# Last layer B of a four-layer kernel: the row gather moved into layer A's inverse, and the last results returned block by block

## The chip, the cores and the metric

The kernel runs on one core of a Trainium2 chip. The metric is the device time of one execution in microseconds (us). Five engines are named as in the profile: PE (TensorE, the matrix engine; PEld is its loading of weights), DVE (VectorE), ACT (ScalarE), POOL (GpSimd) and SP (SyncE). SP does no arithmetic and issues most of the DMA transfers; ACT issues some. Each engine runs its own list of instructions in order, and so does a queue of transfers: an issue that has to wait holds back whatever stands behind it on the same engine.

## What is computed

Four layers run one after the other on x, with 2048 rows of 512 channels: A, B, A, B, each on a layer norm of x and added to it.

```python
x = x + _A_ref(_layernorm(x), A_w_r, A_w_i)      # irfft2(rfft2(x) * W)
x = x + _B_ref(_layernorm(x), ...)               # long convolution of each channel
x = x + _A_ref(_layernorm(x), A_w_r, A_w_i)
x = x + _B_ref(_layernorm(x), ...)

# _B_ref, for each channel d of 512, L = 2048:
K = einsum("dn,dnl,dn->dl", Cc, exp(dt * A * l), dt * Bc).real
y = irfft(rfft(pad(u, 2 * L)) * rfft(pad(K, 2 * L)))[:L] + u * Dskip
```

The kernel does the transforms as matrix products in two steps, because 2048 is split into 128 x 16. The first index is called s1 and lies on the 128 partitions; the second, s2, counts 16 places.

## The kernel before

Layer B of pass r (r = 0 the first layer B, r = 1 the last one) works on two halves e of the channels, 256 each. It has three steps, and between them the data pass through HBM, since each step wants another index on the partitions.

1. `forward_b(r, b, e)`, eight blocks b of two s2 values each: normalise (DVE, L505), transform along s1 (PE, L761), copy from PSUM (ACT, L779) into a buffer of the ring `iy`, and write the rows to the HBM tensor `yd[r][e]` (L782, on SP or ACT).
2. `group_b(r, q, e)`, eight groups q: load the kernel's spectrum `khat` (L865), load the group's rows from `yd` into a buffer of the ring `yi` (L868), transform along s2 (`spectrum`, PE, L803), multiply by the spectrum (DVE, L880, four products), add (POOL, L886, two sums), transform back along s2 (PE, L895), copy (ACT, L904, four copies), and write to the HBM tensor `vd[r][e]` (L905, on ACT).
3. `inv_b(r, b, e)`, eight blocks b: load from `vd` into a buffer of the ring `iy` (L914, on SP), transform back along s1 (PE, L920), add to x (DVE, L926), and in the last layer store the result (L944, one half on SP and one on ACT).

`yd` and `vd` have 8 x 4 x 2 x 2 x 16 x 2 x 256 places, called q, i, a, c, s, w, d. The four indices q, i, a, c together are the partition (128) of steps 1 and 3; a, c, s, w together are that of step 2. So step 1 and step 3 see `pieces`, all partitions and a few s, and step 2 sees `block`, one q:

```python
def pieces(t, b):
    return t.rearrange("q i a c s w d -> (q i a c) s w d")[:, 2 * b:2 * b + 2]
def block(t, q):
    return t[q].rearrange("i a c s w d -> (a c s w) i d")
```

A group therefore needs the rows of all eight blocks of its half, and an inverse block needs all eight groups.

Layer A's second pass ends with sixteen pieces `inv_a(1, s2)` (PE, L730 and L738), with which the sixteen `forward_b(1, b, e)` are interleaved.

The order of all instructions is set by a planner, `Clock.run`: every piece of work is a generator with a rank; at each `yield` it names the engine and the buffers that it needs next, and the events it waits for (`after` an event's planned time, or once it is `emitted`); the planner takes the ready piece of the lowest rank by its own planned times. Buffers are slices of big SBUF tensors: `Ya` (8192 floats in each partition), `Y` (16384), `wk`, `apart`. In pass 1 of layer B, `Ya` holds the rings `yi` and `vo` (four buffers of 1024 floats each), and the second half of `Y` is free by then.

## Time and profile before

| | |
|---|---|
| time, median of 3 runs | 831.39 us (831.05 to 833.83) |
| profiled execution, its own time | 832.5 us |
| its span | 830.7 us |
| mean granted clock of PE | 0.871 |
| PE, DVE, ACT, POOL busy | 625.7, 509.0, 419.8, 279.2 us |
| HBM read, written | 103.47 MB, 60.69 MB |
| transfers Ya<-yd (step 2's loads, both layers B) | 32 of 512 KB, median 10.9 us from issue to landing |
| transfers vd<-Ya | 32 of 512 KB, 6.8 us |
| transfers wk<-vd | 32 of 512 KB, 4.8 us |

Times in the profile count from the span's start. In a row of instructions, `Ya<-yd` reads: written to Ya, read from yd; "x8" is a count. Matrix products in 32-bit floats appear twice in the profile's counts, so that an inverse block's four products are eight records. "To landing" is the time from a transfer's issue to its completion. A wait "A <- B" is idle time of engine and line A, ended by B; "issue" stands where the profile shows nothing that was waited for.

### The profile page before, as it was taken

Reading aid. Unit: us, or ns where it says so; the run is one execution under the profiler, and the core shown is the slowest. Engines: PE = TensorE matmul, PEld = TensorE weight load, DVE = VectorE, ACT = ScalarE, POOL = GpSimd, SP = SyncE. Lnnn points to the kernel's source line nnn. Section 1 sums busy time; section 2 is a strip of 40 time slices with the busy share of each in tenths; the row PEclk is TensorE's granted clock in tenths of the full one; section 3 lists DMA queues with packets and bytes.
Section 4 is the critical chain, followed back from the end, with each engine's and each line's share of the span. In section 5 each row is a group of like instructions: output and inputs, shape, how many; then the busy total and the mean of one; then the engine's idle time right before and its main releaser. Section 6 shows DMA issues by size and latency. Waiting matters only on the chain. (4 is left out here: it accounts for less than half of the span.)

```text
span 830.7 us, 19222 instructions
## 1 busy us (share of the span) xinstructions
PE 625.7 (75%) x7716; PEld 365.4 (44%) x7716; DVE 509.0 (61%) x1019; ACT 419.8 (51%) x755; POOL 279.2 (34%) x275
## 2 busy tenths in 40 slices
PE   4388888678699888885866765699877999577755
PEld 3277555345465333431322322377766534143322
DVE  5966577847757766871432724785877587474533
ACT  5676898888788676752233122085542244332110
POOL 4381345524634411400332404084533000083420
PEclk9699899989899899996686869789997999896776
DMA  9324213623525845399899996600656233799997
GB/s 324 115 86 137 98 44 87 187 84 83 165 68 159 258 148 162 112 347 347 255 332 287 391 386 228 244 0 14 230 203 212 91 124 128 259 323 378 334 309 224
DMA packets 127256, 165.40 MB, mean 199 GB/s; under 512 B 7260, under 2 KB 102240, under 8 KB 127040
## 3 DMA queue, kind: packets, MB, share of 16 engines
q1 hardware_dynamic: 80768, 122.23, 44.4%
q10 hardware_dynamic: 46400, 41.95, 14.8%
q8 instruction: 61, 1.00, 0.5%
q14 instruction: 27, 0.22, 0.1%
HBM read 103.47 MB, written 60.69 MB: 198 GB/s over the span
## 5 line engine op out<-in xcount | busy, mean ns | idle before, releaser
L1131 POOL TENSOR_TENSOR Y<-wk,Y 128x1024 f32<-128x1024 f32 x32 | 65.9, 2059 | 121.9 <-issue 75.7
L904 ACT COPY Ya<-ps 128x256 f32<-128x256 f32 x128 | 38.4, 386 | 126.5 <-PE ps L895 90.2
L886 POOL TENSOR_TENSOR wk<-wk 128x512 f32<-128x512 f32 x32 | 39.8, 1272 | 122.6 <-DVE wk L880 121.8
L761 PE MATMUL ps<-wk,cRb 64*128 64x512 f32 x192 | 63.3, 686 | 18.4 <-DMA wk<-kd 10.7
L880 DVE TENSOR_TENSOR wk<-ps,Y 128x512 f32<-128x512 f32 x64 | 39.4, 682 | 59.2 <-PE ps L803 34.5
L920 PE MATMUL ps<-wk,cRbT 128*64 128x256 f32 x256 | 42.7, 487 | 30.8 <-DMA wk<-vd 26.8
L548 PE MATMUL ps<-cRa,wk 128*128 128x256 f32 x128 | 39.0, 433 | 31.0 <-POOL wk L530 29.7
L880 DVE TENSOR_TENSOR Y<-ps,wk 128x512 f32<-128x512 f32 x64 | 39.2, 681 | 37.3 <-issue 29.6
L730 PE MATMUL ps<-cDaT,apart 128*32 128x256 f32 x256 | 61.3, 391 | 0.2 <-DVE wk L1155 0.2
L886 POOL TENSOR_TENSOR wk<-Y 128x512 f32<-128x512 f32 x22 | 27.4, 1270 | 98.9 <-DVE Y L880 92.2
L1116 DVE SCALAR_TENSOR_TENSOR wk<-wk,ps 128x1024 f32<-128x1024 f32 x32 | 38.9, 1215 | 33.5 <-ACT wk L1114 33.4
L1084 PE MATMUL ps<-wk,Y 96*128 96x512 bf16 x128 | 41.6, 402 | 20.0 <-DVE Y L1127 14.4
L895 PE MATMUL ps<-wk,Y 32*64 32x256 f32 x672 | 37.8, 465 | 20.8 <-POOL wk L886 16.6
L926 DVE TENSOR_TENSOR x<-x,ps 128x256 f32<-128x256 f32 x64 | 25.7, 408 | 39.6 <-PE ps L920 36.7
L803 PE MATMUL ps<-Ya,Y 64*32 64x256 f32 x768 | 37.2, 474 | 15.9 <-issue 7.3
L1100 ACT ACTIVATE Y<-ps 128x1024 f32<-128x1024 f32 x48 | 46.3, 1026 | 5.7 <-PE ps L1084 4.9
L779 ACT COPY wk<-ps 128x512 f32<-128x512 f32 x64 | 34.0, 598 | 30.0 <-PE ps L761 26.8
L1127 DVE TENSOR_TENSOR Y<-ps,Y 128x1024 f32<-128x1024 f32 x32 | 38.9, 1217 | 16.0 <-ACT ps L1120 15.9
L738 PE MATMUL ps<-wk,cRaT 128*128 128x512 f32 x64 | 37.7, 681 | 9.8 <-ACT wk L734 9.0
L920 PEld LDWEIGHTS ps<-wk,cRbT 128*64 128x64 f32 x256 | 22.2, 171 | 51.2 <-issue 28.6
L1144 PEld LDWEIGHTS ps<-Y 128*32 128x32 f32 x2048 | 34.7, 121 | 22.7 <-issue 11.6
L530 POOL TENSOR_TENSOR wk<-wk 128x256 f32<-128x256 f32 x32 | 25.4, 793 | 56.4 <-ACT wk L503 56.1
(204 smaller groups left out, 1571.1 us busy)
## 6 DMA issues: line engine op xcount, KB each, us to landing
Ya<-yd SPq DMA_DIRECT2D x32, 512.0 KB, 10.9
vd<-Ya ACTq DMA_DIRECT2D x32, 512.0 KB, 6.8
wk<-vd SPq DMA_DIRECT2D x32, 512.0 KB, 4.8
yd<-wk SPq DMA_DIRECT2D x20, 512.0 KB, 7.2
yk<-wk ACTq DMA_DIRECT2D x32, 256.0 KB, 2.3
wk<-khat SPq DMA_DIRECT2D x16, 512.0 KB, 9.5
Y<-in_W_dram SPq DMA_DIRECT2D x12, 515.0 KB, 4.9
x<-in_cPa_dram SPq DMA_DIRECT2D x16, 384.0 KB, 4.9
```

The lines of the kernel that those rows point to most:

```text
L548: nc.tensor.matmul(p[:, 0:256], pq[:, 128 * i:128 * i + 128], R2[:, 128 * i:128 * i + 256], start=i == 0, stop=i == 1)
L730: nc.tensor.matmul(p[32 * i:32 * i + 32, o:o + 256], self.folded(r, i)[:, b, s2].rearrange("p g m -> p (g m)"), self.DaT[:, b, :], start=b ...
L761: self.nc.tensor.matmul(p[w], self.Rb[rows, :], x[rows], start=True, stop=True)
L880: nc.vector.tensor_tensor(t[c][:, j], x, kh[:, j, ::-1, :] if c else kh[:, j], op=OP.mult)
L886: nc.gpsimd.tensor_tensor(Z[:, :, c], t[0][:, :, c], t[1][:, :, c], op=op)
L904: nc.scalar.copy(V[:, j, h, :], v[j][h])
L920: nc.tensor.matmul(q[s][64 * w:64 * w + 64], self.RbT[:, w, :], y[:, s, w, :], start=True, stop=True)
L1084: self.nc.tensor.matmul(p, f[:, c:c + 128], self.oh[:k, o:o + 512], start=True, stop=True)
L1100: nc.scalar.activation(m[:, :, 1024:] if i == 2 else m[:, i, :1024], p.rearrange("p (i m) -> p i m", i=2) if i == 2 else p, AF.Exp)
L1116: nc.vector.scalar_tensor_tensor(s, c, MAGIC, p, op0=OP.subtract, op1=OP.subtract)
L1127: nc.vector.tensor_tensor(E[:, 1, :1024], p, m[:, :1024], op=OP.mult)
L1131: nc.gpsimd.tensor_tensor(E[:, 0, :1024], c, m[:, :1024], op=OP.mult)
```

## The change

The gather. In pass 1 the group's rows are no longer loaded per group. Two places of 32 KB per partition, all of `Ya` for half 0 and the second half of `Y` for half 1, take all rows of a half. The new `gather_b(e, i)` reads a quarter: after blocks 2i and 2i+1 have been written, two transfers (w = 0 and 1) bring every eighth partition of the place, 16 partitions with 32 pieces of 1 KB each. So that two blocks make a quarter, the order of s2 in `yd` and `yk` is permuted: block b is written at s = b // 2 + 8 (b % 2) and four further, and the tables follow. A group of pass 1 waits until the four quarters of its half are in, and reads its slice of the place.

The return. The partition order of step 3 becomes (i a c) q, the table `cRbT` follows. A group of half 1 in pass 1 is followed by one transfer that brings its whole block of `vd` into every eighth partition of `Ya` (16 partitions, 32 KB each), and the inverse blocks of that half wait for all eight and read from `Ya`. The other inverse blocks load as before, with the new order of partitions.

The copies out. `vo` has eight buffers of 512 floats instead of four of 1024, in pass 1 six (`vo1`, in `gl` and `apart`); each half of a group's result is written to `vd` by its own transfer of 256 KB. This holds in both passes.

```diff
-RINGB = {"yi": (1024, 4), "vo": (1024, 4)}
+RINGB = {"yi": (1024, 4), "vo": (512, 8)}
...
-    Rt = (np.stack([np.cos(th), -np.sin(th)], -1) / S).reshape(2, 64, 128).transpose(2, 0, 1)
+    Rt = (np.stack([np.cos(th), -np.sin(th)], -1) / S).reshape(2, 64, 8, 16).transpose(3, 2, 0, 1).reshape(128, 2, 64)
...
-    F = np.stack([F.real, F.imag], -3).reshape(8, 2, 2, 2, 64, 2, 32)
+    F = np.stack([F.real, F.imag], -3).reshape(64, 2, 4, 4, 2, 2, 32).swapaxes(2, 3).reshape(8, 2, 2, 2, 64, 2, 32)
...
+        self.place = [a.rearrange("p (g d) -> p g d", d=256) for a in (self.Ya, self.Y[:, 8192:])]
+        self.back = self.Ya
...
-        (self.nc.scalar if b % 2 and e >= r else self.nc.sync).dma_start(self.pieces(self.yd[r][e], b), y)
+        (self.nc.scalar if b % 2 and e >= r else self.nc.sync).dma_start(self.pieces(self.yd[r][e])[:, b // 2 + 8 * (b % 2):][:, :5:4], y)
         self.mark("rows", r, e)
+        self.mark("rows", r, e, b // 2)
...
+    def gather_b(self, e, i):
+
+        yield "SP", self.after(("rows", 1, e, i), 2), self.emitted(("group", 1), 16)
+        src = self.yd[1][e].rearrange("q i a c s w d -> (a c s w) (q i) d")
+        for w in range(2):
+            self.nc.sync.dma_start(self.place[e][2 * i + w::8], src[2 * i + w::8])
+        self.mark("rows in", e)
...
-        yield "SP yi", self.after(("rows", r, e), 8), self.emitted(("added", r), 16)
-        Y = self.w("yi", [128, 2, 2, 256])
-        nc.sync.dma_start(Y.rearrange("p j h d -> p (j h) d"), self.block(self.yd[r][e], q))
+        if r:
+            yield "PE", self.after(("rows in", e), 4), self.emitted(("added", r), 16)
+            Y = self.place[e][:, 4 * q:4 * q + 4].rearrange("p (j h) d -> p j h d", j=2)
+        else:
+            yield "SP yi", self.after(("rows", r, e), 8), self.emitted(("added", r), 16)
+            Y = self.w("yi", [128, 2, 2, 256])
+            nc.sync.dma_start(Y.rearrange("p j h d -> p (j h) d"), self.block(self.yd[r][e], q))
...
-        yield "ACT vo"
-        V = self.w("vo", [128, 2, 2, 256])
         for j in range(2):
+            ring = "vo1" if r else "vo"
+            yield "ACT " + ring
+            V = self.w(ring, [128, 2, 256])
             for h in range(2):
-                nc.scalar.copy(V[:, j, h, :], v[j][h])
-        nc.scalar.dma_start(self.block(self.vd[r][e], q), V.rearrange("p j h d -> p (j h) d"))
+                nc.scalar.copy(V[:, h, :], v[j][h])
+            nc.scalar.dma_start(self.block(self.vd[r][e], q)[:, 2 * j:2 * j + 2], V)
+            self.drop(V)
         self.mark("grouped", r, e)
+        if r and e:
+            yield "SP", self.emitted(("grouped", 1, 0), 8)
+            nc.sync.dma_start(self.back[q::8], self.vd[r][e][q].rearrange("i a c s w d -> (i a c) (s w d)"))
+            self.mark("loaded", r, e)
...
-        yield "SP iy", self.after(("grouped", r, e), 8)
-        y = self.w("iy", [128, 2, 2, 256])
-        nc.sync.dma_start(y, self.pieces(self.vd[r][e], b))
-        self.mark("loaded", r, e)
+        placed = r and e
+        if placed:
+            yield "PE", self.after(("loaded", r, e), 8)
+            y = self.back.rearrange("p (s w d) -> p s w d", w=2, s=16)[:, 2 * b:2 * b + 2]
+        else:
+            yield "SP iy", self.after(("grouped", r, e), 8)
+            y = self.w("iy", [128, 2, 2, 256])
+            src = self.vd[r][e].rearrange("q i a c s w d -> (i a c) q s (w d)")[:, :, 2 * b:2 * b + 2]
+            nc.sync.dma_start(y, src.rearrange("p q s m -> p q (s m)"))
+            self.mark("loaded", r, e)
...
-            out = self.yk[q // 2].rearrange("q i a c s w d -> (q i a c) s w d")
-            nc.scalar.dma_start(out[:, 4 * i:4 * i + 4, w, 128 * (q % 2):128 * (q % 2) + 128], y)
+            nc.scalar.dma_start(self.pieces(self.yk[q // 2])[:, i::4, w, 128 * (q % 2):128 * (q % 2) + 128], y)
...
+        self.ring["vo1"] = self.ring["gl"] + [self.apart[:, 1024:1536], self.apart[:, 1536:]]
...
             for e in range(2):
                 yield 90 + 2 * b + 1.5 + 6 * e, self.forward_b(1, b, e, sa)
+            for e in range(2 * (b % 2)):
+                yield 90 + 2 * b + 1.7 + 6 * e, self.gather_b(e, b // 2)
```

What this moves on the engines is shown at three places. In the rows, yd_112 and yd_115 are `yd[1][0]` and `yd[1][1]`, vd_124 and vd_127 are `vd[1][0]` and `vd[1][1]`; line numbers are those of the kernel that the row is from.

SP before, from the last spectrum loads ahead of layer A's inverse to the first groups of the last layer B:

```order
L865 DMA wk<-khat 128x4x256 x6
L782 DMA yd_112<-wk 128x1024 x3
L782 DMA yd_115<-wk 128x1024
L782 DMA yd_112<-wk 128x1024 x2
L782 DMA yd_115<-wk 128x1024
L782 DMA yd_112<-wk 128x1024 x2
L782 DMA yd_115<-wk 128x1024 x2
L782 DMA yd_112<-wk 128x1024
L868 DMA Ya<-yd_112 128x4x256 x6
L865 DMA wk<-khat 128x4x256 x3
```

The same place on SP in the changed kernel, from the middle of the row writes on (ahead of these rows stand four row writes of half 0, one of half 1, and six gathers):

```order
L784 DMA yd_112<-wk 128x2x512
L784 DMA yd_115<-wk 128x2x512
L784 DMA yd_112<-wk 128x2x512
L798 DMA Ya<-yd_112 16x32x256 x2
L798 DMA Y<-yd_115 16x32x256 x2
L784 DMA yd_112<-wk 128x2x512
L784 DMA yd_115<-wk 128x2x512 x2
L784 DMA yd_112<-wk 128x2x512
L798 DMA Y<-yd_115 16x32x256 x2
L798 DMA Ya<-yd_112 16x32x256 x2
L798 DMA Y<-yd_115 16x32x256 x2
L876 DMA wk<-khat 128x4x256 x10
```

The gathers stand between the row writes; the last six follow the last row write, with half 1's third quarter first, and the ten remaining spectrum loads come behind them.

SP before, near its end:

```order
L914 DMA wk<-vd_124 128x1024
L944 DMA out_dram<-x 64x2x256 x5
L914 DMA wk<-vd_127 128x1024 x5
L944 DMA out_dram<-x 64x2x256
L914 DMA wk<-vd_127 128x1024
```

SP in the changed kernel, from the last spectrum load to its end:

```order
L941 DMA wk<-vd_124 128x1x1024 x4
L926 DMA Ya<-vd_127 16x8192 x2
L971 DMA out_dram<-x 64x2x256 x4
L941 DMA wk<-vd_124 128x1x1024 x4
L926 DMA Ya<-vd_127 16x8192 x4
L971 DMA out_dram<-x 64x2x256 x4
L926 DMA Ya<-vd_127 16x8192 x2
L971 DMA out_dram<-x 64x2x256 x8
```

The loads of vd_127 have become returns of whole blocks, and six of the eight now stand ahead of the second four stores; the last two follow those.

PE before, the end of the program (L803 spectrum, L895 back along s2, L920 inverse along s1):

```order
L803 MATMUL ps<-Ya,wk 32x256 x32
L920 MATMUL ps<-wk,cRbT 64x256 x16
L895 MATMUL ps<-wk 64x256 x16
L803 MATMUL ps<-Ya,wk 32x256 x16
L895 MATMUL ps<-wk 64x256 x16
L803 MATMUL ps<-Ya,wk 32x256 x16
L895 MATMUL ps<-apart,wk 64x256 x16
L920 MATMUL ps<-wk,cRbT 64x256 x8
L895 MATMUL ps<-wk 64x256 x16
L920 MATMUL ps<-wk,cRbT 64x256 x40
```

PE in the changed kernel, the end (L814, L910 and L947 are the same three lines):

```order
L814 MATMUL ps<-Y,wk 32x256 x32
L910 MATMUL ps<-wk,Y 64x256 x16
L947 MATMUL ps<-wk,cRbT 64x256 x16
L910 MATMUL ps<-wk,Y 64x256 x16
L910 MATMUL ps<-apart,Y 64x256 x16
L910 MATMUL ps<-wk 64x256 x32
L947 MATMUL ps<-wk,cRbT 64x256 x16
L910 MATMUL ps<-apart,wk 64x256 x16
L910 MATMUL ps<-wk 64x256 x16
L947 MATMUL ps<-Ya,cRbT 64x256 x32
```

All spectra now stand ahead of the inverse blocks of half 0; two groups stand behind the second four of those, and half 1's eight inverse blocks, read from Ya, are one run at the end.

More of the change, by code (lines that the diff above doesn't have):

```diff
@@ L781, in forward_b, with pieces @@
         yield "SP"
-        (self.nc.scalar if b % 2 and e >= r else self.nc.sync).dma_start(self.pieces(self.yd[r][e], b), y)
+        (self.nc.scalar if b % 2 and e >= r else self.nc.sync).dma_start(self.pieces(self.yd[r][e])[:, b // 2 + 8 * (b % 2):][:, :5:4], y)
         self.mark("rows", r, e)
+        self.mark("rows", r, e, b // 2)
     @staticmethod
-    def pieces(t, b):
-        return t.rearrange("q i a c s w d -> (q i a c) s w d")[:, 2 * b:2 * b + 2]
+    def pieces(t):
+        return t.rearrange("q i a c s w d -> (q i a c) s w d")
+    def gather_b(self, e, i):
[4 more added lines that the diff above has]
+        self.mark("rows in", e)
     @staticmethod
@@ L872, in group_b @@
         self.spectrum(gi, [Y[:, j] for j in range(2)], X)
-        self.drop(Y)
+        self.drop(*() if r else (Y,))
         names = ("t1b", "t2b", "Zb") if r else ("t1", "t2", "Z")
@@ L920, in inv_b @@
                 nc.tensor.matmul(q[s][64 * w:64 * w + 64], self.RbT[:, w, :], y[:, s, w, :], start=True, stop=True)
-        self.drop(y)
+        self.drop(*() if placed else (y,))
         yield "DVE"
```

## The prediction

> **What bounds the kernel now.** I first read the profile's slices, to see which stages fill the DMA engines.
>
> ```profile
> DMA  9324213623525845399899996600656233799997
> GB/s 324 115 86 137 98 44 87 187 84 83 165 68 159 258 148 162 112 347 347 255 332 287 391 386 228 244 0 14 230 203 212 91 124 128 259 323 378 334 309 224
> ```
>
> One slice is 20.8 us. Slices 31 to 33 (counted from 0), layer A's second inverse, keep DMA at two to three tenths; from slice 35 on, the last layer B, it stands at nine. The table by stretches says it in numbers (columns: busy time and count of PE, PEld, DVE, ACT, POOL, then granted clock, DMA share, GB/s):
>
> ```profile
> 663.00:716.00 53.00, 49.76 (x464) 20.14 (x454) 40.37 (x103) 24.25 (x50) 0.00 (x0) 1.00 0.35 140
> 720.00:780.00 60.00, 43.27 (x832) 20.38 (x832) 30.84 (x51) 14.40 (x48) 29.87 (x24) 0.76 1.04 356
> 718.00:804.00 86.00, 60.53 (x1088) 29.15 (x1088) 45.39 (x80) 19.20 (x64) 39.78 (x32) 0.80 0.98 332
> 804.00:831.00 27.00, 11.98 (x64) 6.59 (x64) 6.74 (x16) 0.00 (x0) 0.00 (x0) 0.63 0.79 248
> ```
>
> In 663 to 716 PE is busy 49.8 of 53 us and DMA a third. In 718 to 804, the sixteen groups, no engine is over 70% busy and DMA is full, at 332 GB/s (356 in its first 60 us). The waits of the stretch from 716 on agree: DVE's products starve, and the label "issue" there hides a PE that waits for spectra input.
>
> ```profile
> DVE Y L880 <- issue: 29.6, 4, 10.8
> PE ps L803 <- issue: 7.3, 1, 7.3
> PE ps L920 <- DMA wk<-vd: 12.4, 4, 6.8
> ```
>
> What moves there is listed by the DMA view of 716 to 831:
>
> ```profile
> DMA packets 29389, 35.84 MB, mean 312 GB/s; under 512 B 1472, under 2 KB 27072, under 8 KB 29376
> ...
> Ya<-yd SPq DMA_DIRECT2D x16, 512.0 KB, 11.6
> vd<-Ya ACTq DMA_DIRECT2D x16, 512.0 KB, 7.9
> wk<-vd SPq DMA_DIRECT2D x16, 512.0 KB, 3.7
> wk<-khat SPq DMA_DIRECT2D x10, 512.0 KB, 7.1
> out_dram<-x SPq DMA_DIRECT2D x16, 128.0 KB, 3.1
> out_dram<-x ACTq DMA_DIRECT2D x16, 128.0 KB, 4.4
> yd<-wk SPq DMA_DIRECT2D x1, 512.0 KB
> yd<-wk ACTq DMA_DIRECT2D x1, 512.0 KB, 2.9
> ```
>
> A transfer of 512 KB is 0.524 MB, so the reads of the groups' rows (Ya<-yd) are 8.39 of 35.84 MB in the stage that is full. The start of the stage and its end, from the timeline and the chain that ended last:
>
> ```profile
> 713.60 1.99 PE L761 MATMUL ps<-wk,cRb 64*128 64x512 f32 x8 [2.15 <-DVE wk L505]
> 715.83 0.32 SPq L782 DMA_DIRECT2D yd<-wk  x1
> 716.82 0.33 ACTq L782 DMA_DIRECT2D yd<-wk  x1
> 718.59 8.10 SPq L868 DMA_DIRECT2D Ya<-yd  x6
> 722.91 4.02 PE L803 MATMUL ps<-Ya,Y 64*32 64x256 f32 x72 [7.32 <-issue]
> 724.95 4.87 DVE L880 TENSOR_TENSOR Y<-ps,wk 128x512 f32<-128x512 f32 x8 [10.85 <-issue]
> 798.15 1.75 PE L895 MATMUL ps<-wk 32*64 32x256 f32 x32
> 800.77 0.38 ACTq L905 DMA_DIRECT2D vd<-Ya  x1
> ...
> 800.77 2.98 DMA vd<-Ya
> 803.81 4.78 DMA wk<-vd
> 818.96 5.24 DMA wk<-vd
> 826.35 0.42 DVE x L926
> ```
>
> The last rows leave at 716.8, the first spectrum starts at 722.9, the last block's result is sent at 800.8, the first of the eight loads for half 1's inverse lands at 808.6, the last at 824.2, and after the last add, at 826.8, the final stores fill 3.9 us up to 830.7.
>
> **The change, part by part.** *The row writes* keep their bytes; each piece of 4 KB becomes two of 2 KB. Most packets of the full stage above are under 2 KB and still move at 356 GB/s, so the price is nothing: in 663 to 716 two thirds of the DMA time are spare, and without that cover the packets' row would still allow the full rate.
>
> *The sixteen yi reads* go; sixteen gathers of the same 512 KB come, each into 16 partitions. On SP they stand between the row writes and wait for rows to land. SP has room for that; it waits for ACT's copies most of that stage:
>
> ```profile
> SPq L782 <- ACT wk L779: 66.3, 11, 20.0
> yd<-wk SPq DMA_DIRECT2D x12, 512.0 KB, 2.6
> ```
>
> Five such waits of 2.6 us stand against 66 us idle, so nothing queued behind them is late by them: not the next row writes, nor the ten khat loads that now stand behind the last gather, since six are loaded early and the seventh group comes some 15 us into the stage (six groups at DVE's 2.44). If the iy ring of four blocks in the last burst of five row blocks, PE can be late by the time of two gathers, 0 to 4 us; I take 0, as PE had a hole of 2.15 us there anyhow. Ten gathers (quarters 0 to 2 of half 0, 0 and 1 of half 1) have their rows before 716; six (half 1's quarter 2, then quarter 3 of both) have not. So the bytes after 716 fall by 10 x 0.524 = 5.2 MB, to 30.6 MB.
>
> *The price of a transfer to 16 partitions* no row shows. One end is the full rate: 0.524 MB / 356 GB/s = 1.47 us. For the other I take transfers that touch few partitions, the stores to kd (L1164, 256 KB out of 32), beside two out of all 128 (stores to spe, 128 KB; the rows yd above, 512 KB). First the row of kd, then that of spe:
>
> ```profile
> DMA to landing us min/median/max: 3.1/5.5/6.3
> ...
> DMA to landing us min/median/max: 1.7/1.7/1.7
> ```
>
> From 128 partitions 128 KB land in 1.7 us and 512 KB in 2.6, so about 1.4 us are fixed. From 32 partitions 256 KB take 3.1, of which 1.7 move the bytes: 3.4 us for 512 KB. Below 1.47 nothing reaches. I take 1.95 us, a quarter of the way, since the slow row is of four such transfers back to back, and here they are 14 of 512 KB (six gathers, eight returns), 7.3 of 30.6 MB, a quarter of what moves, with others between them. The ends for fourteen: 20.6 us and 47.6 us; taken 27.3.
>
> [...]
>
> *Start of the groups.* From 716.2 on come two row writes (1.05 MB / 356 = 2.9 us), two gathers of half 1 and two of half 0 (4 x 1.95 = 7.8), and 1.4 us until the last has landed: 728.3 instead of 722.9. All four quarters must be in before the first group, where one block was enough; that is 5.4 us lost.
>
> The rows for the work after a product, of 716 to 831 by groups:
>
> ```profile
> L886 POOL TENSOR_TENSOR wk<-Y 128x512 f32<-128x512 f32 x22 | 27.4, 1270 | 98.9 <-DVE Y L880 92.2 <-PE ps L920 6.6
> L904 ACT COPY Ya<-ps 128x256 f32<-128x256 f32 x64 | 19.2, 386 | 64.8 <-PE ps L895 50.3 <-DMA out_dram<-x 10.1 <-DMA wk<-khat 4.4
> ```
>
> *The groups.* Engines alone: products start 2.0 us after the first spectrum; DVE takes 4.87 us for two groups, 39.0 for sixteen; eight inverse blocks of half 0 cost it two adds of 0.42 each, 6.7; then POOL, PE and ACT once more, 2.5 + 1.75 + 1.5. That path ends at 781.8, and 3.0 for the write and 4.8 for the return give 789.6. DMA: two gathers and eight returns (10 x 1.95 = 19.5), and khat 5.24, vd written 8.39, vd read for half 0 4.19 and half 0's output 2.10, together 19.92 MB / 356 = 56.0. So 728.3 + 75.5 = 803.8: DMA stays the bound by 14 us. Sixteen more vd writes cost ACT 0.38 us an issue, 6.1 in this stage; its 64.8 idle us hide that, and uncovered it would be those 6.1. In the first layer B and in the kernel table's stores (yk) bytes and piece sizes stay, only addresses and the halving of vd change: zero, with 2 us either way kept for the range.
>
> Two inverse blocks at a full clock:
>
> ```profile
> 783.91 1.95 PE L920 MATMUL ps<-wk,cRbT 128*64 128x256 f32 x16 [1.77 <-DVE x L926]
> ```
>
> *The tail.* The eight inverse blocks of half 1 wait for all eight returns, then need no load of their own: PE's 12.0 us of the last stretch in one piece, a last add of 0.42 and 3.9 of stores, 16.3. Before, from the first vd landing (808.6) to the end it was 22.1. The clock there was 0.63; at full clock PE would need 7.8 (1.95 for 16 records at 783.9, two blocks), which I keep for the range.
>
> *Sum.* 803.8 + 16.3 = 820.1 against the span of 830.7: 10.6 us less. The profiled execution took 832.5 us, 1.8 above its span and 1.1 above the median of 831.39; from the median, 831.39 - 10.6 = 820.8, so 821. A cross-check: 30.6 MB at the mean of 312 GB/s is 98 us after 716, 814, and 6.7 us more for the fourteen dearer transfers, 821.
>
> **The rivals.** *A, 16-partition transfers at full rate:* fourteen cost 20.6 us instead of 27.3, so 814. The packets' row (under 2 KB at 356 GB/s) speaks for it, the 3.1 us row against.
>
> DMA at its best, last column:
>
> ```profile
> 740.00:750.00 10.00, 7.28 (x154) 3.42 (x144) 5.29 (x9) 3.29 (x12) 5.58 (x5) 1.00 1.09 381
> 750.00:760.00 10.00, 5.87 (x104) 2.17 (x112) 4.19 (x8) 1.51 (x6) 4.07 (x4) 0.65 1.09 383
> ```
>
> *B, DMA is no longer the bound:* if the mixture runs at the 380 to 390 GB/s which it held at its best, and gathers hide, the engines' path sets it: 789.6 + 16.3 = 805.9 of span, 807 from the median. Against it: 14 us must vanish.
>
> *C, slower, by one mechanism:* transfers into 16 partitions are slow enough to eat the gain. It decides at 27.3 + 10.6 = 37.9 us for fourteen, 2.7 us each. At half rate (2.94 us) they take 41.2: 835. At 3.4 us: 841. The 3.1 us row speaks for it; against it, that row's transfers came four in a row, and here a vd write or a row write runs beside most. [...]
> *D, the gain goes into queueing:* SP issues returns ahead of the second four loads of half 0, and PE's last two groups stand behind those; if that costs the 8 to 10 us which SP's wait for them can take (four loads and two returns, 3.1 MB at 356), it ends near 830.
>
> **How the numbers follow.** Forecast 0.40 (816 to 827), A 0.18, B 0.10, C 0.22, D 0.10. A measurement can tell about 0.3% from no change; within it are 829 to 834. Faster: forecast, A, B and half of D, 0.73. Same: half of D and the near end of C, 0.09. Slower: the rest of C, 0.18. The range of 806 to 838 leaves out half of B and C's far end; the likeliest case alone has 816 to 827.
>
> **What would show it.** DMA share of 663 to 716 near 0.6 with PE's busy time unchanged; first spectrum at 727 to 730; 30 to 31 MB after 716; gathers landing in 2.5 to 6 us, returns in 3 to 6; DVE's idle time in the groups under 15 us; the last inverse in one piece of 8 to 12 us after a wait for the last return. Wrong would make it: gathers landing in 8 us or more with nothing else moving, the first spectrum after 735, or PE's inverse of layer A held up by row buffers.

## The result, and the profile after

The changed kernel takes **872.35 us** (median of 4 runs, 869.24 to 876.36), against 832.61 (831.05 to 836.62) for the kernel before on the same chip: ratio **1.0472, 95% interval 1.0410 to 1.0535**, slower by 39 us. I had predicted 821 (806 to 838).

The profiled execution took 869.24 us with a span of 867.4, against 832.5 and 830.7 before. First the stretches, with the columns as in the prediction:

```profile
663.00:716.00 53.00, 50.18 (x467) 20.59 (x468) 42.19 (x107) 23.43 (x47) 0.00 (x0) 0.99 0.77 191
738.00:805.00 67.00, 48.30 (x904) 21.63 (x904) 42.65 (x72) 13.84 (x43) 34.93 (x28) 0.91 0.79 225
805.00:840.00 35.00, 19.65 (x184) 10.11 (x184) 3.37 (x8) 6.85 (x22) 4.98 (x4) 0.65 0.86 216
840.00:867.00 27.00, 10.06 (x64) 6.36 (x64) 6.74 (x16) 0.00 (x0) 0.00 (x0) 0.63 0.63 166
```

Read the last two columns against each other. In layer A's inverse the DMA share went from 0.35 to 0.77, but the rate only from 140 to 191 GB/s. In the groups the share is still 0.79, at 225 GB/s instead of 332. The transfer engines are busy and move little: the transfers themselves have become slow.

The end of the chain of waits (start, duration, what):

```profile
710.11 11.41 DMA yd<-wk
722.69 3.59 DMA yd<-wk
726.92 11.38 DMA Ya<-yd
...
785.01 9.83 DMA wk<-vd
...
817.78 8.62 DMA wk<-vd
826.44 1.71 PE ps L947 x8
828.15 1.23 PE ps L910 x28
...
837.18 7.09 DMA vd<-Y
845.62 6.66 DMA Ya<-vd
```

A row write takes 11.4 us where 2.6 was usual, and a gather 11.4. Two loads of half 0 (8.6 and 9.8 us) stand in the chain, with the group work of half 1 behind their inverse blocks.

PE, the first spectrum, where its last groups stand, and the last inverse:

```profile
738.38 4.33 PE L814 MATMUL ps<-Ya,Y 64*32 64x256 f32 x72 [19.40 <-DMA Ya<-yd]
...
805.17 2.24 PE L910 MATMUL ps<-apart,Y 32*64 32x256 f32 x24 [5.61 <-ACT Y L920]
807.18 5.39 PE L910 MATMUL ps<-wk 32*64 32x256 f32 x64
819.04 1.97 PE L947 MATMUL ps<-wk,cRbT 128*64 128x256 f32 x8 [6.47 <-DMA wk<-vd]
...
835.03 2.24 PE L910 MATMUL ps<-wk 32*64 32x256 f32 x24 [4.28 <-ACT apart L920]
852.49 10.06 PE L947 MATMUL ps<-Ya,cRbT 128*64 128x256 f32 x64 [15.21 <-DMA Ya<-vd]
```

DVE's 64 products of the last layer, before (L880) and in the changed kernel (L895), and the changed kernel's writes to vd, one of which follows the last in the chain. Behind the count stand the shortest, median and longest duration in ns, then the first and the last start:

```profile
L880 DVE TENSOR_TENSOR Y<-ps,wk x64: 677/680/692, 725.0 to 792.8; 128x512 f32<-128x512 f32 x64
L895 DVE TENSOR_TENSOR Y<-ps,wk x64: 679/681/693, 740.4 to 802.6; 128x512 f32<-128x512 f32 x64
L921 ACTq DMA_DIRECT2D vd<-Y x22: 366/366/1031, 748.2 to 838.6; - x22
```

This splits the 36.7 us of span. The first spectrum starts at 738.4 instead of 722.9: 15.5. From there to the last vd write it is 100.2 us (838.6) instead of 77.9 (800.8): 22.3. From that write to the end it is 28.8 instead of 29.9: the returns were to shorten this part, and it is 1.1 shorter. The 22.3 are not lost in the products. From the first to the last they take 62.2 us instead of 67.8; it is the way from the last product to the last vd write that grew, from 8.0 to 36.0 us.

SP shows what stands there and why the tail gained so little (L926 are the returns, L941 the loads of half 0, L971 stores):

```profile
783.15 2.46 SPq L941 DMA_DIRECT2D wk<-vd  x4
785.72 13.24 SPq L926 DMA_DIRECT2D Ya<-vd  x2
805.89 5.70 SPq L971 DMA_DIRECT2D out_dram<-x  x4
813.72 4.60 SPq L941 DMA_DIRECT2D wk<-vd  x4
818.42 17.10 SPq L926 DMA_DIRECT2D Ya<-vd  x4
835.75 9.17 SPq L971 DMA_DIRECT2D out_dram<-x  x4
845.02 1.19 SPq L926 DMA_DIRECT2D Ya<-vd  x2
```

The second four loads of half 0 are issued 30 us after the first four, behind two returns and four stores. PE holds the groups of half 1 behind the inverse blocks of these loads, and the last two returns wait for those groups.

### The profile page after: what moved, and what is told of

Same layout as the page of the kernel before. It is cut to its first block, busy times and chain, and to the rows that moved or that the text cites. A ratio compares the mean times of both kernels' runs of the same rounds, so it can differ in the third digit from the quotient of the medians.

```text
span 867.4 us, 19244 instructions
## 1 busy us (share of the span) xinstructions
PE 630.3 (73%) x7716; PEld 366.8 (42%) x7716; DVE 511.0 (59%) x1019; ACT 422.3 (49%) x755; POOL 279.3 (32%) x275
## 3 DMA queue, kind: packets, MB, share of 16 engines
q10 hardware_dynamic: 48448, 41.95, 14.7%
## 5 line engine op out<-in xcount | busy, mean ns | idle before, releaser
L763 PE MATMUL ps<-wk,cRb 64*128 64x512 f32 x192 | 63.5, 703 | 20.1 <-DMA wk<-kd 11.5
L895 DVE TENSOR_TENSOR wk<-ps,Y 128x512 f32<-128x512 f32 x64 | 39.6, 683 | 53.1 <-PE ps L814 24.1
L895 DVE TENSOR_TENSOR Y<-ps,wk 128x512 f32<-128x512 f32 x64 | 39.6, 683 | 42.2 <-issue 24.4
L947 PE MATMUL ps<-wk,cRbT 128*64 128x256 f32 x192 | 40.5, 562 | 32.2 <-DMA wk<-vd 28.0
L814 PE MATMUL ps<-Ya,Y 64*32 64x256 f32 x640 | 33.1, 486 | 29.8 <-DMA Ya<-yd 25.9
L920 ACT COPY Ya<-ps 128x256 f32<-128x256 f32 x64 | 20.7, 375 | 60.0 <-PE ps L910 28.2
L1154 DVE TENSOR_TENSOR Y<-ps,Y 128x1024 f32<-128x1024 f32 x32 | 39.0, 1219 | 15.8 <-ACT ps L1147 15.7
L920 ACT COPY Y<-ps 128x256 f32<-128x256 f32 x44 | 14.2, 375 | 63.3 <-PE ps L910 53.6
L910 PE MATMUL ps<-wk,Y 32*64 32x256 f32 x672 | 35.7, 412 | 11.5 <-ACT Ya L920 11.3
L740 PE MATMUL ps<-wk,cRaT 128*128 128x512 f32 x64 | 36.7, 663 | 9.8 <-ACT wk L736 9.1
```

The costliest lines, as they stand in the source:

```text
L740: nc.tensor.matmul(q, self.RaT, Y4, start=True, stop=True)
L763: self.nc.tensor.matmul(p[w], self.Rb[rows, :], x[rows], start=True, stop=True)
L814: self.nc.tensor.matmul(X[j][o:o + 32, 256 * c:256 * c + 256], G[i, j, 2 * h + c, :], y[j][i, h, :], start=True, stop=True)
L895: nc.vector.tensor_tensor(t[c][:, j], x, kh[:, j, ::-1, :] if c else kh[:, j], op=OP.mult)
L910: nc.tensor.matmul(v[j][h][64 * a:64 * a + 64], gi[o:o + 32, j, 4 + 2 * c:6 + 2 * c, :].rearrange("p a m -> p (a m)"), Z[o:o + 32, j, c, : ...
L947: nc.tensor.matmul(q[s][64 * w:64 * w + 64], self.RbT[:, w, :], y[:, s, w, :], start=True, stop=True)
```

## The experiments

Each time is a median; the ratio is to runs of the kernel before on the same chip in the same study, and kernels of different studies are compared by their ratios. One per cent is 8.3 us.

**micro: the transfers by themselves.** Eight transfers of 512 KB (4.19 MB) in each section, from the same HBM layout, each section ended by a small copy on DVE that waits for all of them.

```python
g[c::8] <- src[c::8]            # gathers: 16 partitions eight apart, 1 KB pieces
g[:, 4*c:4*c+4] <- rows[c::8]   # the same HBM rows, into 128 partitions
g[c:c+106:7] <- src[c::8]       # 16 partitions seven apart (7 transfers)
P[q::8] <- yd[q]                # returns: 16 partitions, 32 KB each
P[...] <- (q i a c), (i a c) q  # the vd loads, old and new order of partitions
g[c::4] <- src[c::4]            # 32 partitions four apart, 4 x 1 MB
g[16*c:16*c+16] <- src[...]     # 16 partitions side by side
```

> This kernel leaves the layers out: it only moves 4 MB per section between HBM and SBUF, eight transfers of 512 KB each, and a DVE copy ends every loading section. Theory 1 (the partitions of a transfer set its rate): the gathers into 16 partitions eight apart take about 2.7 us each (22 us for eight), the same source rows into 128 partitions 1.4 us each (11 to 13), returns of 32 KB into 16 partitions eight apart also 2.7 each (22), 16 partitions side by side about twice as long again (40), seven apart between 13 and 22; the inverse's loads with partitions (q i a c) 1.4 each, with partitions (i a c) q more, up to 2.7, since the transfer's outermost dimensions no longer match. Theory 2 (the gather's rows in HBM, 1 KB every 8 KB, are slow to read): gathers and the same rows into 128 partitions both take 2.7 us each, returns 1.4, and the two forms of the inverse's load the same. Row writes in two pieces of 2 KB: as fast as 4 KB pieces by both.

DVE's copies; the bracket is the time since the copy before, that is, the section's time:

```profile
73.75 0.19 DVE L25 COPY junk<-P 128x32 f32<-128x32 f32 x1 [24.68 <-DMA P<-yd]
89.70 0.19 DVE L25 COPY junk<-P 128x32 f32<-128x32 f32 x1 [15.76 <-DMA P<-yd]
107.75 0.19 DVE L25 COPY junk<-P 128x32 f32<-128x32 f32 x1 [17.86 <-DMA P<-yd]
130.28 0.19 DVE L25 COPY junk<-P 128x32 f32<-128x32 f32 x1 [22.34 <-DMA P<-yd]
144.56 0.20 DVE L25 COPY junk<-P 128x32 f32<-128x32 f32 x1 [14.09 <-DMA P<-yd]
165.22 0.19 DVE L25 COPY junk<-P 128x32 f32<-128x32 f32 x1 [20.46 <-DMA P<-yd]
180.10 0.20 DVE L25 COPY junk<-P 128x32 f32<-128x32 f32 x1 [14.70 <-DMA P<-yd]
221.21 0.19 DVE L25 COPY junk<-P 128x32 f32<-128x32 f32 x1 [40.91 <-DMA P<-yd]
```

In the order of the list: gathers 24.7 us (170 GB/s), the same HBM rows into 128 partitions 15.8 (266), seven apart 17.9 for seven (206), returns 22.3 (188), vd loads old 14.1 (298) and new 20.5 (205), 32 partitions four apart 14.7 (285), 16 side by side 40.9 (103). The scattered rows in HBM cost little: 15.8 us into 128 partitions, where pieces of 4 KB take 14.1. Which partitions are written costs more: a gather is 3.1 us, where the same rows into 128 partitions are 2.0 a transfer; a return is 2.8. And the new form of the vd loads, which I had taken as "only addresses", is 0.8 us a load dearer; the reason that theory 1 gave for it was not tested. Row writes in pieces of 2 KB landed after 5.5 us (median) against 4.9 in pieces of 4 KB; they had no copy behind them, so this shows only that their price is small. Of the transfers into 16 partitions those side by side are the slowest, at 103 GB/s against 170 eight apart and 206 seven apart; into 32 four apart it is 285. The sections show these rates, not what makes them.

**e_gather, e_ret, e_late: the parts in the kernel.** The first leaves the returns away and loads vd in the old form; the second leaves the gathers away and returns into Y; the third is the changed kernel with the returns as pieces of their own, behind all loads of half 0.

```diff
 e_gather
-        if r and e:                        # the return
+        if False:
-        placed = r and e
+        placed = False
+            nc.sync.dma_start(y, self.pieces(self.vd[r][e])[:, 2 * b:2 * b + 2])
 e_ret
-        if r:                              # a group waits for "rows in" and reads its place
+        if False:
-                yield 90 + 2 * b + 1.7 + 6 * e, self.gather_b(e, b // 2)
 e_late
+    def return_b(self, q):
+        yield "SP", self.after(("block", q)), self.emitted(("grouped", 1, 0), 8), self.emitted(("loaded", 1, 0), 8)
+        self.nc.sync.dma_start(self.back[q::8], ...)
```

> The gathers alone; half 1's results are loaded by block as before, with the partition order of before. Theory 1 and queueing (the gathers cost the first spectrum 15 us and return most of it in the groups, and the rest of the loss is made at the end by the returns and by what SP's order puts ahead of what): 828 to 842 us. Rival (the slow gathers are the whole loss): 860 to 872 us.

> No gathers: each group loads its rows as before; returns, new partition order of the inverse's loads and halved vd writes stay, with the place of the returns in the second half of Y. Theory 1 and queueing: the end is as bad as in the changed kernel, 845 to 860 us. Rival (gathers are the whole loss): 824 to 834 us.

> The changed kernel, with the returns as pieces of their own and emitted on SP only after all eight loads of half 0's inverse; PSUM banks of a group are then free for the planner before its return. If SP's order at the end costs the 20 us: 846 to 856 us. If it is the transfers' rate that costs them, whatever the order: 865 to 876 us.

Measured: e_gather 840.22 us, ratio 1.0147 (1.0107 to 1.0187), as expected of slow gathers. e_ret 871.54, 1.0523 (1.0467 to 1.0580): dearer than either theory said, and no better than both changes together. e_late 863.80, 1.0421 (1.0366 to 1.0476), against 1.0472: the place of the returns on SP, with the PSUM banks that a group holds until its return is issued, is worth about 4 us, with intervals that overlap. That lies between what the two theories gave. e_gather, which has the halved copies too, is 12 us slower than before, although the sixteen loads of rows have left the groups.

**e_load, e_noret, e_two: form of the loads against returns.** The kernel before with the new form of all vd loads; the changed kernel without returns; the changed kernel with its returns, but all other vd loads in the old form (a second table).

```diff
 e_load
-        nc.sync.dma_start(y, self.pieces(self.vd[r][e], b))
+        src = self.vd[r][e].rearrange("q i a c s w d -> (i a c) q s (w d)")[:, :, 2 * b:2 * b + 2]
+        nc.sync.dma_start(y, src.rearrange("p q s m -> p q (s m)"))
 e_noret: the two lines "if False" and "placed = False" of e_gather, not its third
 e_two
-            src = self.vd[r][e].rearrange("q i a c s w d -> (i a c) q s (w d)")[:, :, 2 * b:2 * b + 2]
+            nc.sync.dma_start(y, self.pieces(self.vd[r][e])[:, 2 * b:2 * b + 2])
```

> The kernel before, with one thing changed: step 3's partition order is (i a c) q and the table of the inverse follows, so that all 32 loads of vd (both layers B) have the changed kernel's form. By the theory that this form is itself slow (the measurement by itself had 8 such loads in 20.4 us against 14.1 in the old form, 0.8 us more each), the eight loads of half 1 in each layer, which nothing hides, cost 6.3 us a layer, and the 16 others up to 12.6 together where DMA is full: 837 to 852 us, with loads of 8 us or more from issue to landing in the last layer. By the rival, that the form is hidden or only slow when it runs alone and the queueing of returns is what costs, it stays at 826 to 831.

> The changed kernel without its returns: gathers, halved copies and the new form of all vd loads stay, half 1's inverse blocks load from vd again. With the gathers alone at 840, the theory that the load's form costs what is left gives 846 to 860 us; the theory that returns and their place in the queue and in PE's order cost it gives 838 to 845.

> The changed kernel with the loads of vd other than the returns in the old partition order (a second table for them); gathers, returns and halved copies stay. If the load's form is what costs beside the gathers, 848 to 860 us, and half 0's four-load bursts end in 5 to 6 us where they took over 8. If the returns do (their rate into 16 partitions, SP's order, PE's order), 864 to 874.

Measured: e_load 839.83, 1.0113 (1.0071 to 1.0155); e_noret 856.81, 1.0282 (1.0215 to 1.0349); e_two 861.39, 1.0337 (1.0272 to 1.0403). From issue to landing, after 716 in e_load (before: 3.7; I had expected 8 or more):

```profile
wk<-vd SPq DMA_DIRECT2D x16, 512.0 KB, 6.5
```

e_load and e_noret are where the theory of the form put them, e_two a little above. Three estimates of the form agree: 1.1% alone, 1.4% from e_gather to e_noret, 1.4% from e_two to the changed kernel. It is 9 to 11 us, in a line that changed nothing but the order of partitions.

**e_best: gathers at the full rate.** As e_gather, but each quarter is one transfer of 1 MB into 32 partitions four apart (285 GB/s in micro, where the transfers of e_gather go at 170 and the old vd loads at 298); the order of the rows in yd follows.

```diff
-        for w in range(2):
-            self.nc.sync.dma_start(self.place[e][2 * i + w::8], src[2 * i + w::8])
+        self.nc.sync.dma_start(self.place[e][i::4], src[i::4])
```

> The gathers alone (loads of vd old, no returns), but each quarter comes as one transfer of 1 MB into 32 partitions four apart instead of two of 512 KB into 16 partitions eight apart. Measured by itself that went at the full rate (14.7 us for 4 MB, against 24.7). If the rate into 16 partitions is why the groups start late and inverse A is held up, the first spectrum starts at 726 to 730 instead of 733.3 and a DMA share in 663 to 716 of 0.6 instead of 0.9; the time is 829 to 835 us. If it isn't, about 840 as with the gathers alone.

Measured: 834.14, 1.0008 (0.9969 to 1.0046). PE, DVE and POOL have the same order as in e_gather, so I put the 11.5 us between the two down to the rate; but the edit also halves the number of gathers and cuts the row writes into pieces of 1 KB. PE's first spectrum, in e_gather and here:

```profile
733.27 6.41 PE L814 MATMUL ps<-Ya,Y 64*32 64x256 f32 x104 [22.16 <-DMA Ya<-yd]
```

```profile
723.66 4.03 PE L818 MATMUL ps<-Ya,Y 64*32 64x256 f32 x72 [12.31 <-issue]
```

PE is idle 12.3 us ahead of it instead of 22.2 (before: 7.3); the starts don't compare with before's 722.9, since layer A's last row block ended 4 us earlier in both traces. In layer A's inverse the rate rose from 217 to 248 GB/s while the DMA share fell from 0.87 to 0.77. It was not the 0.6 that I expected. Still, no gain against before is left.

**e_half, e_half1, e_half2: the halved copies.** All three are the kernel before with a group's result written in two transfers of 256 KB. In e_half each half is a step of the planner (as in the changed kernel), in e_half1 both are one step, and in e_half2 the planner counts the two writes as one, which gives every instruction on PE, DVE, POOL and SP exactly the order of before.

```diff
 e_half, in group_b; vo has eight buffers of 512
-        yield "ACT vo"
         for j in range(2):
+            yield "ACT vo"
+            V = self.w("vo", [128, 2, 256])
             ...
+            nc.scalar.dma_start(self.block(self.vd[r][e], q)[:, 2 * j:2 * j + 2], V)
 e_half1
+        yield "ACT vo vo"
+        V = [self.w("vo", [128, 2, 256]) for _ in range(2)]
 e_half2; vo has four buffers of 1024; four copies, then
+        for j in range(2):
+            nc.scalar.dma_start(self.block(self.vd[r][e], q)[:, 2 * j:2 * j + 2], V[:, j])
```

> The kernel before, with one thing changed: vo has eight buffers of 512 floats, and each half of a group's result goes to vd by its own transfer of 256 KB, in both layers B. If the halving is as free as the prediction took it (ACT has idle time in the groups), the time stays within 0.3% of before. If the doubled issues matter (16 more of 0.38 us on ACT per layer, and smaller transfers), it is 1 to 6 us slower. With the gathers alone 12 us slower than before and 6 us of that given back by the transfers into 32 partitions, up to 3 of the rest could be this.

> The kernel before with the halved vo and the two writes of 256 KB per group, but with the copies of a group as one step of the planner: it takes two halves at once, makes four copies and two writes. The transfers, their sizes and ACT's instructions are those of the kernel with halved copies alone (851 us); what differs is PE's order, where back transforms of two or three groups stand together again, as before, and no longer one by one behind the next group's spectrum. Theory (order): 829 to 838 us, and DVE's products no longer 8.3 us apart. Rival (the smaller writes or their issues themselves are dear): 846 to 855.

> The kernel before with a group's write to vd split in two of 256 KB, as in the changed kernel, but with every instruction of PE, DVE, POOL and SP in exactly the order of before (vo keeps its four whole buffers, ACT makes four copies and then the two writes; the planner counts the two as one). The kernel with copies in one step (848 us) had not brought the old order back: its products are still 8.3 us apart between 766 and 783. If order is the cause of the 17 us of the halved copies, this is at 829 to 836 us; if the smaller transfers or the second issue on ACT are, at 844 to 853.

Measured: e_half 851.19, 1.0201 (1.0143 to 1.0258); e_half1 848.44, 1.0182 (1.0123 to 1.0240); e_half2 832.40, 1.0030 (0.9994 to 1.0066). So the small writes cost at most 0.7%; with the same writes in another order it is 17 us. e_half1 had missed: it was to bring the old order back and did not. How the order costs it is in e_half's groups. First DVE's products, then POOL's sums, then PE (L803 spectrum, L895 back along s2):

```profile
757.62 2.48 DVE L880 TENSOR_TENSOR Y<-ps,wk 128x512 f32<-128x512 f32 x4 [5.79 <-POOL wk L886]
765.90 2.48 DVE L880 TENSOR_TENSOR Y<-ps,wk 128x512 f32<-128x512 f32 x4 [5.80 <-POOL apart L886]
774.18 2.48 DVE L880 TENSOR_TENSOR Y<-ps,wk 128x512 f32<-128x512 f32 x4 [5.80 <-POOL wk L886]
```

```profile
763.38 2.49 POOL L886 TENSOR_TENSOR apart<-Y 128x512 f32<-128x512 f32 x2 [5.80 <-issue]
```

```profile
758.96 0.64 PE L803 MATMUL ps<-Ya,Y 64*32 64x256 f32 x8 [3.21 <-DVE Y L880]
760.15 1.93 PE L803 MATMUL ps<-Ya,Y 64*32 64x256 f32 x24 [0.56 <-DVE Y L880]
762.02 2.01 PE L895 MATMUL ps<-apart,wk 32*64 32x256 f32 x32
```

It is a closed loop; the brackets name two of its links, and the third (POOL and the place for its sums) is "issue" here and follows from the code. A product waits for POOL to free its buffers; POOL waits for a place for its sums, which only the back transform frees; PE has put the next spectrum ahead of that; and the spectrum waits for a bank that the product frees. One turn: 1.34 us of product, 3.06 of spectrum, 1.36 of back transform, 2.52 of POOL, 8.28 us a group where DVE and POOL need 2.5. In e_half1 the loop runs the other way round, with the back transform ahead of the only spectrum that could feed DVE, and products start 8.3 us apart as well. With the order of before (e_half2) they come two at a time, 10.5 to 11.1 us a pair:

```profile
760.77 4.88 DVE L882 TENSOR_TENSOR Y<-ps,wk 128x512 f32<-128x512 f32 x8 [5.82 <-issue]
771.24 4.88 DVE L882 TENSOR_TENSOR Y<-ps,wk 128x512 f32<-128x512 f32 x8 [5.59 <-issue]
782.35 4.88 DVE L882 TENSOR_TENSOR Y<-ps,wk 128x512 f32<-128x512 f32 x8 [6.24 <-issue]
```

**e_one: the changed kernel with a group's copies as one step** (the edit of e_half1 in it).

> The changed kernel with only that edit: a group's copies out as one step. Gathers, returns, the new form of loads, sizes and numbers of transfers stay. If the order that the two steps bring is worth 17 us, as in the kernel before with halved copies alone, 850 to 860 instead of 872; if in the changed kernel the late rows and the slow transfers set the time whatever PE's order, 866 to 874.

Measured: 863.61, 1.0407 (1.0345 to 1.0470), against 1.0472: some 5 us, and the intervals overlap. That lies between what the two theories gave. The loop fills e_half's trace from 749.3 to 774.2, three steps of 8.3 us where e_half2 has 5.2 to 5.6, so it explains 8 to 9 of the 17 us; the rest was not traced. In the changed kernel it hardly stands: from 762.9 to 789.5 the products start 2.9 to 7.0 us apart. In e_ret it stands again; the products start at 753.50, 761.78, 770.06 and 778.34, 8.3 us apart, which is likely a part of why returns alone cost more than I expected there.

**e_ret16, e_pair0, e_pair1: the returns.** e_ret16 is e_best with returns as pieces of their own, eight of 512 KB into 16 partitions. e_pair0 has four of 1 MB into 32 partitions instead, with the same order on PE. e_pair1 is e_pair0 with a group's copies as one step; e_best1 is the same edit in e_best.

```diff
 e_ret16
+        self.nc.sync.dma_start(self.back[g::8], self.vd[1][1][g].rearrange("i a c s w d -> (i a c) (s w d)"))
 e_pair0
+        self.nc.sync.dma_start(self.back[g::4], self.vd[1][1][2 * g:2 * g + 2].rearrange("q i a c s w d -> (q i a c) (s w d)"))
 e_pair1, e_best1
+        yield f"ACT {ring} {ring}"
+        V = [self.w(ring, [128, 2, 256]) for _ in range(2)]
```

> The same kernel as the one with four returns of 1 MB, with the same order on PE, but with eight returns of 512 KB into 16 partitions eight apart. By the half rate measured alone (22.3 us for eight against 14.7 for 4 MB into 32 partitions), the returns take 7 to 8 us more of the transfer engines, and what of it shows is 4 to 8 us above that kernel. If the rate is hidden there, the two are equal within 2 us, and the banks or the queue are what made the returns of the changed kernel dear.

> The kernel with gathers of 1 MB into 32 partitions, old loads of vd in half 0 and in the first layer B, and returns again, but as four transfers of 1 MB: each brings two groups of half 1 into 32 partitions four apart, in pieces of 32 KB, issued as a piece of its own, so that a group's PSUM banks come free before it. If the rate into 16 partitions and the banks held by a group are why returns cost 21 us (the changed kernel with the old loads against the gathers alone), returns now cost nothing and shorten the tail: 820 to 832 us, last inverse blocks in one run after the last return. If returns cost because the queue on SP puts them ahead of loads and stores, 840 to 850.

> Gathers and four returns of 1 MB into 32 partitions, old loads elsewhere, with a group's copies as one step. If order was what kept the whole plan from its gain (837 with two steps), 812 to 826 us, below the kernel without returns by the tail's loads. If returns cost by their place on SP ahead of half 0's loads and stores, it stays above that kernel by 3 us or more.

> Gathers of 1 MB into 32 partitions, no returns, old loads, with a group's copies as one step. If the step's order took the gathers' gain (834 with two steps), this is faster than before: 815 to 826 us, with all products done by 770 and the last vd write by 793. If the gathers have no gain to give, 828 to 836.

Measured: e_ret16 846.56, 1.0164 (1.0120 to 1.0207); e_pair0 837.46, 1.0035 (1.0004 to 1.0067), between its two theories; e_pair1 833.75, 1.0021 (0.9992 to 1.0051); e_best1 829.04, 0.9993 (0.9957 to 1.0028). Returns into 16 partitions instead of 32 cost 10.7 us (e_ret16 less e_pair0), more than the 4 to 8 I expected; micro has no return into 32, and their places on SP differ too. From e_two to e_ret16 (gathers at full rate, returns as pieces of their own) it is 14 us. Into 32 partitions the returns still bring nothing: e_pair0 is 2 us above e_best, e_pair1 2 to 5 above e_best1, by ratios and medians. e_best1 is itself where the theory without a gain put it: one step in place of two is worth 1 to 5 us there, not the 10 that I looked for. But its trace shows that the groups did become shorter:

```profile
L899 DVE TENSOR_TENSOR Y<-ps,wk x64: 678/682/694, 729.1 to 773.4; 128x512 f32<-128x512 f32 x64
```

The products take 44.3 us instead of 67.8 and end 19 us sooner than before, though they start 4 us later. The last vd write leaves at 790.8, 10 us sooner, as PE's last groups stand behind inverse blocks of half 0 and ACT's copies behind stores. From there to the end of the span it is 32.8 us instead of 29.9. This span, 823.6 us, is that of the fastest of twelve runs; over all of them nothing is left.

**e_order, e_top: the order of the tail.** No inverse block of half 0 on PE before the last group of half 1 has gone back; in e_best and in e_pair1.

```diff
+        self.mark("back", r, e)            # in group_b, after the back transform
-        yield "PE p:h p:t"
+        yield "PE p:h p:t", self.emitted(("back", 1, 1), 8 * r * (1 - e))   # in inv_b
```

> The kernel with gathers of 1 MB into 32 partitions and without returns, with one thing changed: no inverse block of half 0 is put on PE before the last group of half 1 has gone back along s2. In that kernel's trace the last product ended at 777 us, but the last vd write left at 800, because five groups stood on PE behind inverse blocks, and ACT's copies behind stores that waited for their adds. If this order is where the gathers' gain went, the last vd write leaves at 785 to 790 and the time falls by 5 to 10 us, to 822 to 829. If the stage is bound by the transfers after all, the tail gets what the groups lose, half 0's loads and stores come later and run into half 1's, and the time stays at 830 to 836 or rises.

> Gathers and four returns of 1 MB into 32 partitions, old loads elsewhere, copies as one step, and no inverse block of half 0 on PE before the last group of half 1. In the kernel without the last condition the last return was issued on SP at 810.7, behind four stores that waited for the adds of half 0's last block. If the place of the returns on SP is what they cost, the last return now leaves some 10 us earlier and the time is 812 to 826 us. If the tail is bound by what is left to move (half 0's loads and all stores come after the groups), 828 to 838.

Measured: e_order 831.26, 0.9987 (0.9951 to 1.0024), no gain against before, as the theory of a tail bound by its transfers had it. e_top 829.21, 0.9962 (0.9925 to 0.9998): 3 us faster than before, if it is faster at all, since the interval ends just below 1 and this is the best of eighteen kernels. It is short of the 812 to 826 that I expected. SP and PE at e_top's end:

```profile
803.47 0.37 SPq L951 DMA_DIRECT2D wk<-vd  x1
803.93 0.65 SPq L981 DMA_DIRECT2D out_dram<-x  x1
804.67 0.54 SPq L951 DMA_DIRECT2D wk<-vd  x1
805.41 0.59 SPq L981 DMA_DIRECT2D out_dram<-x  x1
806.06 0.60 SPq L937 DMA_DIRECT2D Ya<-vd  x1
```

```profile
790.22 3.29 PE L916 MATMUL ps<-wk 32*64 32x256 f32 x32 [2.54 <-ACT apart L927]
...
813.88 8.81 PE L957 MATMUL ps<-Ya,cRbP 128*64 128x256 f32 x64 [2.36 <-DMA Ya<-vd]
```

PE has finished the last group at 793.5, but the last return leaves at 806.1, behind two loads and two stores of half 0. That this place on SP holds the rest of the gain is only read from the rows; a kernel with the last return ahead of them was not run.

## Why the prediction was wrong, point by point

The sign was wrong: forecast 821, measured 872. My range ended at 838, the dearest rival at 841. One of the signs that I had named came, a first spectrum after 735 (738.4). The first step that failed is the price of a transfer into 16 partitions; the next are the vd loads and the row writes, both put at nothing, and the place of the gain.

- *The price of a transfer into 16 partitions* was the first term that failed. I took 1.95 us, between 1.47 and 3.4; micro shows 3.1 for a gather and 2.8 for a return. Fourteen then take 6 x 3.1 + 8 x 2.8 = 41.0 us instead of 27.3. That is rival C, with its break-even of 2.7 passed, and its half-rate sum of 41.2 was right to a fraction for transfers measured by themselves; the 835 made from it was not, because that sum had nothing else in it. Its half of 356 GB/s, 178, was an assumption that no run shows as a half; micro has 170 GB/s for gathers and 188 for returns, beside 298 for the old vd loads. The only row that bore on it (kd, 3.1 us) pointed there, and I put it aside for a guess.
- *Row writes at nothing, and PE late by 0 to 4 us, taken as 0*: it failed with the rate. Row writes queue among slow gathers, and ACT's copy stood 7.3 us until a row buffer was free (8.2 in e_gather; e_best has no such wait):

```profile
721.59 1.07 ACT L781 COPY wk<-ps 128x512 f32<-128x512 f32 x2 [7.26 <-DMA yd<-wk]
```

- *Start of the groups at 728.3.* The mechanism, four quarters instead of one block, was right, the size was not. At full rate PE's idle time ahead of the first spectrum went from 7.3 to 12.3 us (e_best), 5.0 more, where the same sum with 1.47 us a gather gives 3.5. In the changed kernel the sum with 3.1 us gives 10.0; PE was idle 12.1 us longer, and as its last row block had ended 3.4 us later (719.0 instead of 715.6), the start was 738.4.
- *The vd loads, "only addresses", zero within 2 us*: failed, 9 us alone and 11 in the changed kernel. Partitions and pieces, by which I priced transfers, gave no difference here, as both stayed; what changed is the distance in HBM between the places that neighbouring partitions read, and I put that at nothing without measuring it.
- *The halving, zero*: right for the transfers and issues (e_half2), wrong for what comes with it. A second planner step moves PE's spectra and back transforms against each other, and in the kernel before that alone is 17 us (e_half). I had shown PE's new order for the end of the program only, and read no price from it. In the changed kernel some 5 us of it are left (e_one).
- *DMA as the bound of the groups, 30.6 MB after 716*: in the changed kernel this failed. 33.15 MB moved after 716, since gathers that were issued in time had not moved, at 219 GB/s where the sum had 356. At full rate it was half right. With the loads of rows out of the groups, e_best1's products take 2.8 us a group, near the 2.44 of the engines' path, so those loads, with the order that went with them, did hold them before. But a shorter group stage was not a shorter program: 1.0008 in e_best, 0.9993 in e_best1. The time from the last product to the last vd write was 8.0 us before and is 17.4 in e_best1, and moving half 0's inverse behind the last group (e_order) gains nothing either. What binds there is not settled; in e_best1 DMA is busy 0.94 from 780 to 800, at 297 GB/s.
- *The tail, 16.3 us*: right from where I measured it. From the last return's landing (845.62 + 6.66 = 852.3) to the end it is 15.1, with the inverse in one piece of 10.1 us. But that return landed 13.7 us after the last vd write, where the first of the loads had landed after 7.8.
- *Rival D, returns ahead of the second four loads*: the mechanism is in SP's rows, as told. Undone in e_late it gives 4 us, where I had 8 to 10. Its error was to be set against a gain, when it comes on top of the other losses.
- *Two readings beside the sum.* PE is busy 60.5 of 86 us in 718 to 804, 70.4% and so just over the 70% said, and 1.47 us a transfer was no floor: at the 383 GB/s of the rows under rival B 512 KB take 1.37. Neither moves the forecast by much.

The account, by ratios: rate of the gathers 11.5 us (e_gather less e_best), form of the loads 11 (changed kernel less e_two), returns 16 (changed kernel less e_noret), together 38.5 of the 39. That the sum comes out is no proof of its parts: e_best, e_gather, e_noret and the changed kernel are one chain of steps from 1.0008 to 1.0472. What is measured is that the form costs the same with returns and without. The halved copies and the later start lie inside e_best, against the shorter groups. Of the 16 us of the returns, 10.7 are their 16 partitions instead of 32, by e_ret16 and e_pair0, and their place on SP with the held banks 4 by e_late, both measured in kernels that differ otherwise. Not settled is why the new form of the loads is slow, and how much of the 36.0 us from the last product to the last vd write is PE's order rather than the late loads in it.

## What to carry to other kernels

Price a transfer by the partitions that it touches and by the order of partitions against memory, not by its bytes: measure each new form by itself before the plan is built on it, since here each of the three new forms took 45 to 59% longer for its bytes than the nearest form measured (20.46 and 22.34 us against 14.09, 24.68 against 15.76). A DMA share near one is a reason to take bytes out of a stage, but not a promise that the program becomes shorter: here the products could be made to end 19 us sooner and the end did not move, so follow the work behind the stage to the end, in the order in which the engines would do it. And where a planner sets the order, a change that is free in itself can cost more than it saves by the order that comes with it, so try it once with the order held as it was.

## What the runs showed of the hardware

- In micro, rows of 1 KB spread over HBM by 8 KB were read at 266 GB/s, close to the 298 of 4 KB pieces, when they went into 128 partitions, and at 170 into 16 partitions eight apart. The same 4.19 MB in rows of 1 KB went at 285 into 32 partitions four apart, with 4 KB between the rows of a transfer, and at 103 into 16 side by side, with sixteen rows next to each other.
- In micro, loads into all 128 partitions in pieces of 4 KB went at 205 GB/s where neighbouring partitions read places 512 KB apart, and at 298 where these are 32 KB apart. All 128 partitions are written in both, and the pieces are the same. No run here says why.
- With its order held, splitting a group's 512 KB write into two of 256 KB cost at most 0.7% (e_half2, 1.0030, 0.9994 to 1.0066).
